# Start bytes of the SBUF tiles in a retention, GLU and SwiGLU kernel: three small edits that shift them

## The chip, the core and the metric

The kernel runs on one core of a Trainium2 chip. The metric is device time in microseconds (us) of one execution. Three runs of the kernel before took 668.92, 669.10 and 670.97 us; their median is 669.1 us. Names used below: PE is TensorE (matmuls), PEld its weight loads, DVE is VectorE, ACT is ScalarE, POOL is GpSimd, SP is the queue that issues most DMAs.

## The reference

Three steps in a row, all in float32:

```
# 1. retention, batch 2, heads 8, sequence 768, head size 64
state = gamma[h] * state + outer(k[t], v[t])
y[t]  = (1 / sqrt(64)) * q[t] @ state
# 2. GLU on x = y as 1536 tokens x 512:  (x @ w_a) * (x @ w_b) @ w_out        (512 -> 1536 -> 512)
# 3. RMS norm with gain rms_g, then SwiGLU: (silu(xn @ w_gate) * (xn @ w_val)) @ w_out
```

## The kernel before

**Retention.** The recurrence is cut into 12 chunks of 128 tokens (6 per batch). A chunk has scores (L363), an update of the state (L379), the part that comes from the state (L389) and the part from the chunk itself (L399). These are float32 matmuls on small tiles. The chunks run first; the last seven are interleaved with the first three units of step 2 (`BETWEEN`), and the last of them is done by 79 us, in group 0.

**The two networks.** A float32 number is split into two float32r numbers, hi and lo, and each product is three float32r matmuls: hi*hi, hi*lo, lo*hi. Each network has 12 slices of 128 hidden features. Of each slice there are three weight pieces (s = 0, 1 for the two up projections, s = 2 for the down projection), 128 x 512 each, held as a `wh` and a `wl` tile. Tokens go in 3 blocks of 512. A *unit* is one slice for one block: two halves of 12 up matmuls (L170 to L172: moving operand `xh` or `xl`, in the second network `nh` or `nl`; stationary operand a 128 x 128 cut of `wh` or `wl`) and 12 down matmuls of an earlier unit. In the first network (L214 to L216) the down weights are stationary and `hh`, `hl` move; in the second (L218 to L220) `hh`, `hl` are stationary and the down weights `wh`, `wl` move. So each unit has 36 matmuls of 512 columns, and there are 72 units, 2592 such matmuls.

**Groups and buffers.** Slices go in groups of 3; a group runs its 3 slices for the 3 blocks, 9 units, before the next begins. There are 8 groups, 0 to 3 in the first network and 4 to 7 in the second. The weight tiles form a ring of six slices. Slices 0, 1, 2 of the ring lie in the pool `wp`, slices 3, 4, 5 ("the last three") in the pool `wq`. Groups 0, 2, 4, 6 read `wp`, groups 1, 3, 5, 7 read `wq`. A down projection runs two to three units behind its up projection, so the first 24 or 36 down matmuls in a group still read the other pool's weights.

**Beside TensorE.** ACT, DVE and POOL turn the raw weights into `wh` and `wl` (`conv_w`; raw loads by SP, the last steps are ACT L136 for `wh` and DVE L138 for `wl`), form `h`, `hh`, `hl` (L194 to L197), and gather the sums (L241 to L245). `norm` (L249 and on) does the RMS norm of a block; it keeps per-token numbers in five tiles of 128 x 4: `me`, `t`, `r`, `rh`, `rl`. POOL spreads `rh` and `rl` into `d` (L278), which PE multiplies with `ones` (L284).

**Order.** The program runs in the order in which it is written. `unit` issues up halves, steps of the conversions and of the norm, and the down matmuls due; `BEGIN` says in which unit a conversion starts. Each engine takes its instructions in that order; waits are for the tiles that an instruction reads or overwrites.

**Where tiles start.** In each partition of SBUF the tiles stand one behind another, pool by pool, each taking its bytes rounded up to 32. The first tile, `rg_sb` (16 bytes), starts at 16,512, a multiple of 128, so the next starts 32 bytes into a line of 128. Nearly all that follow are a multiple of 128 bytes long and keep that. The exceptions are in two places, which use the same memory at different times:

- in the retention's pool `ac`: `dk_sb` (6 x 8 numbers, 192 bytes) and `gq_sb` (6 x 4 numbers, 96 bytes). Behind them stand `warm` and the retention's working tiles `q`, `k`, `qd`, `vd`, `p`, `sd`, `dq`.
- in the pool `yp`, opened when the retention is done: the five norm tiles of 16 bytes, 32 each, 160 in all. Behind them stands `wq`.

| tiles | start before | in a line of 128 |
|---|---|---|
| x and n tiles (`xh`, `xl`, `nh`, `nl`) | 18,080 and on | 32 |
| `wp`: slices 0 to 2 of the ring | 67,232 and on | 32 |
| `g`, `h`, `hh`, `hl`, `raw`, `u`, `v`, `z`, `acc` | 104,096 and on | 32 |
| `sq`, `d` | 175,776 and 183,968 | 32 |
| retention's `q`, `k`, `qd`, `vd`, `p`, `sd`, `dq` | 162,752 and on | 64 |
| `wq`: slices 3 to 5 of the ring | 188,224 and on | 64 |

Of the kernel before, what the change touches and what calls it, by code (L numbers as in the profile page):

```python
# [7 lines left out]
F32 = mybir.dt.float32  # L8
# [7 lines left out]
B, H, S, D = 2, 8, 768, 64  # L16
P = 128
# [5 lines left out]
CPB = S // C  # L23
NP = H // 2
# [3 lines left out]
NB = NT // TB  # L28
CPT = TB // C
TPB = TB // P  # L30
# [9 lines left out]
BEGIN = {0: (1, 1), 1: (1, 1), 2: (0, 1)}  # L40
BEGIN |= {i: (i in (10, 13, 16, 19, 22), 1) for i in (*range(3, 34), *range(39, 66))}
LAG = 3
SIGN = -(1 << 31)

PARTS = KD, TPB
# [3 lines left out]
def retention_glu_swiglu(ctx: ExitStack, tc: tile.TileContext, qk, kv, dq, tri, dk, gq, eye, w1, w2, rg, out):  # L49
# [19 lines left out]
    cst = ctx.enter_context(tc.tile_pool(name="cst", bufs=1))  # L69
# [9 lines left out]
    ones = cst.tile([P, P], F32R, name="ones")  # L79
    ones32 = cst.tile([P, P], F32, name="ones32")  # L80
    ident = cst.tile([P, 1, P], F32, name="ident")

    xs = {}

    def x_tiles(j, what):
        hi = xp.tile([P, KD, TB], F32R, tag="xh", name=f"{what}h{j}")
        lo = xp.tile([P, KD, TB], F32R, tag="xl", name=f"{what}l{j}")
        xs[what, j] = (hi, lo)
# [18 lines left out]
    def conv_w(i):  # L107
# [15 lines left out]
        nc.vector.tensor_scalar(ui, ui, 3, 0x7FFFFFFF, op0=ALU.logical_shift_left, op1=ALU.bitwise_and)  # L123
        nc.vector.scalar_tensor_tensor(ui, upper, SIGN, ui, op0=ALU.bitwise_and, op1=ALU.bitwise_or)
        nc.vector.tensor_scalar(zi, ui, -(1 << 23), None, op0=ALU.bitwise_and)  # L125
# [24 lines left out]
    def step(todo=beside):  # L150
        for g in list(todo):
            if next(g, g) is g:
                todo.remove(g)
# [21 lines left out]
    def up(i):  # L175
# [13 lines left out]
        def second():  # L189
            b = up_half(i, 1)  # L190
            h = hp.tile([P, TB], F32, tag="h", name=f"h{i}")
            hh = hp.tile([P, TB], F32R, tag="hh", bufs=LAG, name=f"hh{i}")
            hl = hp.tile([P, TB], F32R, tag="hl", bufs=LAG, name=f"hl{i}")
            nc.vector.tensor_tensor(h, b, gate[0], op=ALU.mult)  # L194
# [27 lines left out]
    def collect(i):  # L222
        ffn, g, j, f = units[i]
        if f % GRP < GRP - 1:
            return
        if g == 0:
            acc[ffn, j] = (yp if j else y0).tile([P, *((TPB, DM) if ffn else (KD, TB))], F32, tag=f"acc{j}", name=f"acc{ffn}_{j}")
        for m in range(PARTS[ffn]):
            collect_part(ffn, g, j, m)
        if ffn == 0 and g == NG - 1:  # L230
            norming.append(norm(j))
# [17 lines left out]
    def norm(j):  # L249
        y = acc[0, j]  # L250
        sq = yp.tile([P, KD, TB], F32, tag="sq", name=f"sq{j}")
        d = yp.tile([P, 2, TB], F32R, tag="d", name=f"d{j}")
        me, t, r, rh, rl = (yp.tile([P, TPB], F32, tag=w, name=f"{w}{j}") for w in ("me", "t", "r", "rh", "rl"))
        nc.scalar.activation(sq[:, 0:2, :], y[:, 0:2, :], AF.Square)
        nc.scalar.activation(sq[:, 2:4, :], y[:, 2:4, :], AF.Square)
        yield
        yield
        nc.vector.tensor_tensor(sq[:, 0:2, :], sq[:, 0:2, :], sq[:, 2:4, :], op=ALU.add)
        nc.vector.tensor_tensor(sq[:, 0, :], sq[:, 0, :], sq[:, 1, :], op=ALU.add)
        for _ in range(4):  # L260
            yield
        ms = sp.tile([P, TB], F32, tag="S", name=f"ms{j}")
        for c in range(TPB):
            nc.tensor.matmul(ms[:, c:c + 1], sq[:, 0, c * P:(c + 1) * P], ones32[:, 0:1], start=True, stop=True)
        yield

        nc.vector.tensor_scalar(me, ms[:, 0:TPB], 1.0 / DM, 1e-6, op0=ALU.mult, op1=ALU.add)
        nc.scalar.activation(t, me, AF.Sqrt)
        yield
        nc.vector.reciprocal(r, t)  # L270
        nc.vector.tensor_tensor(t, r, r, op=ALU.mult)
        nc.vector.scalar_tensor_tensor(t, t, -0.5, me, op0=ALU.mult, op1=ALU.mult)
        nc.vector.scalar_tensor_tensor(r, t, 1.5, r, op0=ALU.add, op1=ALU.mult)
        nc.vector.tensor_copy(rh.bitcast(F32R), r)
        nc.vector.tensor_tensor(rl, r, rh, op=ALU.subtract)

        for i, w in enumerate((rh, rl)):
            nc.gpsimd.tensor_tensor(d[:, i].rearrange("p (c t) -> p c t", t=P), ident.to_broadcast([P, TPB, P]), w[:, :, None].to_broadcast([P, TPB, P]), op=ALU.mult)  # L278
        yield
        yield  # L280
        yield
        rb = sp.tile([P, TB], F32, tag="S", name=f"rb{j}")
        for i in range(2):
            nc.tensor.matmul(rb, ones, d[:, i], start=(i == 0), stop=(i == 1))  # L284
        yield
        x_tiles(j, "n")
        hi, lo = xs["n", j]
        for e in range(0, KD, 2):
            for k in (e, e + 1):
                nc.vector.scalar_tensor_tensor(y[:, k, :], y[:, k, :], rg_sb[:, k:k + 1], rb, op0=ALU.mult, op1=ALU.mult)  # L290
            nc.scalar.copy(hi[:, e:e + 2, :], y[:, e:e + 2, :])
            yield
            for k in (e, e + 1):
                nc.gpsimd.tensor_tensor(lo[:, k, :], y[:, k, :], hi[:, k, :].bitcast(F32), op=ALU.subtract)
        normed.add(j)
# [3 lines left out]
    def unit(i):  # L299
# [3 lines left out]
        for n, f in enumerate(up(i)):  # L303
# [6 lines left out]
            if n == 0:  # L310
                due(i - (LAG if i < 4 * GRP else LAG2))
                step()

    def due(i):
        while nd[0] <= i:
            for m in range(PARTS[units[nd[0]][0]]):
                down(nd[0], m)
            collect(nd[0])
            nd[0] += 1

    with tc.manual_schedule():

        with ExitStack() as att:
            ac = att.enter_context(tc.tile_pool(name="ac", bufs=1))
# [3 lines left out]

            dq_sb = ac.tile([P, NP, C], F32, name="dq_sb")
            tri_sb = ac.tile([P, 1, C], F32, name="tri_sb")  # L330
            dk_sb = ac.tile([P, CPB, H], F32, name="dk_sb")
            gq_sb = ac.tile([P, CPB, NP], F32, name="gq_sb")
            st = sp.tile([P, B, NP, D], F32, name="st")
            qk_t, kv_t = {}, {}

# [76 lines left out]
            w = ps.tile([P, P], F32, tag="A", name="w")  # L412
# [52 lines left out]
        yp = ctx.enter_context(tc.tile_pool(name="yp", bufs=1))  # L465
# [59 lines left out]
```

## Time and profile before

| | us |
|---|---|
| median of the three runs | 669.1 |
| the profiled execution | 669.5 |
| its span in the trace | 667.7 |
| PE busy in it | 653.4 |
| DVE, ACT, POOL busy | 427.1, 255.6, 166.3 |

The profile is one execution. Busy time of PE is modelled at a matmul's end: neighbouring matmuls are pipelined and their spans overlap (one is drawn about 0.39 us long, the next starts about 0.23 us after it). So for TensorE the distance from start to start is what is read here, over a counted number of matmuls, and not the length of one. Idle time of an engine other than the one that bounds costs nothing by itself.

### The profile page before, as it was taken

What the parts mean: (1) busy time and instruction counts of PE and PEld (TensorE: products, weight loads), DVE (VectorE), ACT (ScalarE), POOL (GpSimd) and SP (SyncE); (2) the same over time, 40 slices, a digit from 0 to 9 for tenths busy, and PEclk for the clock granted to TensorE, in tenths of its full rate; (3) what the DMA queues carried; (4) which work ended last, traced back from release to release, by engine and by line L of the source; (5) the groups of instructions that cost most, each with busy time, mean ns of one, the idle gap of its engine ahead of it and who ended that gap; (6) DMA issues with size and microseconds to landing.
All of it is one profiled execution on the core that took longest, in us unless ns stands there. A gap on an engine that the chain in (4) does not pass through costs nothing.

```text
span 667.7 us, 8594 instructions
## 1 busy us (share of the span) xinstructions
PE 653.4 (98%) x3342; PEld 533.3 (80%) x3342; DVE 427.1 (64%) x703; ACT 255.6 (38%) x436; POOL 166.3 (25%) x118
## 2 busy tenths in 40 slices
PE   7699999999999999999999999999999999999997
PEld 6588888888888888888887888888888888888885
DVE  4988545564876976665765657665665775775333
ACT  3555324444344443333443454443333333332110
POOL 3766211121221222211133225111111111111000
PEclk7899999999999999999999999999999999999999
DMA  9866121231332332222210012122122222200111
GB/s 353 299 234 242 36 64 64 63 96 31 95 95 64 95 95 68 67 61 61 65 60 0 1 31 64 63 64 64 63 64 63 64 63 64 64 31 1 63 64 63
DMA packets 16601, 54.47 MB, mean 82 GB/s; under 512 B 2224, under 2 KB 2736, under 8 KB 16560
## 3 DMA queue, kind: packets, MB, share of 16 engines
q1 hardware_dynamic: 15840, 53.42, 24.8%
q8 instruction: 26, 0.43, 0.3%
q10 hardware_dynamic: 720, 0.50, 0.2%
q14 instruction: 15, 0.12, 0.1%
HBM read 50.76 MB, written 3.15 MB: 81 GB/s over the span
## 4 chain that ended last, share of the span: by engine, by line
PE 91%; DVE 5%; DMA 2%; ACT 1%; POOL 1%; issue 1%; ACTq 0%; DVEq 0%; POOLq 0%
PE a L170 19%; PE a L171 19%; PE a L172 19%; PE y L218 5%; PE y L219 5%; PE y L220 5%; PE y L215 5%; PE y L214 5%; PE y L216 5%; PE ya L399 1%; DMA q<-in_qk 1%; PE ya L389 1%; DMA tri_sb<-in_tri 1%; PE sc L363 1%; DVE acc L241 1%; DVE p L365 1%
## 5 line engine op out<-in xcount | busy, mean ns | idle before, releaser
L126 POOL TENSOR_TENSOR v<-v,z 128x512 f32<-128x512 f32 x72 | 113.2, 1572 | 397.4 <-DVE z L125 397.4
L194 DVE TENSOR_TENSOR h<-a,g 128x512 f32<-128x512 f32 x72 | 49.8, 691 | 154.6 <-PE a L172 154.4
L171 PE MATMUL a<-xl,wh 128*128 128x512 f32 x288 | 113.5, 394 | 0.0
L170 PE MATMUL a<-xh,wh 128*128 128x512 f32 x288 | 113.3, 393 | 0.0
L171 PE MATMUL a<-nl,wh 128*128 128x512 f32 x288 | 113.2, 393 | 0.0
L170 PE MATMUL a<-nh,wh 128*128 128x512 f32 x288 | 113.0, 392 | 0.0
L172 PE MATMUL a<-nh,wl 128*128 128x512 f32 x288 | 112.9, 392 | 0.0
L172 PE MATMUL a<-xh,wl 128*128 128x512 f32 x288 | 112.6, 391 | 0.0
L136 ACT CAST wh<-u 128x512 fp32r<-128x512 f32 x72 | 44.7, 620 | 146.0 <-DVE u L134 145.8
L195 ACT CAST hh<-h 128x512 fp32r<-128x512 f32 x72 | 44.7, 620 | 124.4 <-DVE h L194 124.0
L134 DVE TENSOR_TENSOR u<-u,v 128x512 f32<-128x512 f32 x72 | 53.4, 741 | 28.6 <-POOL v L126 28.6
L170 PEld LDWEIGHTS a<-xh,wh 128*128 128x128 f32 x288 | 54.0, 188 | 13.0 <-issue 0.5
L170 PEld LDWEIGHTS a<-nh,wh 128*128 128x128 f32 x288 | 54.1, 188 | 12.4
L171 PEld LDWEIGHTS a<-nl,wh 128*128 128x128 f32 x288 | 54.1, 188 | 12.2
L172 PEld LDWEIGHTS a<-xh,wl 128*128 128x128 f32 x288 | 54.1, 188 | 12.2
L172 PEld LDWEIGHTS a<-nh,wl 128*128 128x128 f32 x288 | 54.1, 188 | 12.1
L171 PEld LDWEIGHTS a<-xl,wh 128*128 128x128 f32 x288 | 54.1, 188 | 11.8
L138 DVE TENSOR_TENSOR wl<-u,wh 128x512 fp32r<-128x512 f32 x72 | 58.6, 814 | 0.7 <-ACT wh L136 0.7
L215 PE MATMUL y<-hl,wh 128*128 128x512 f32 x144 | 56.8, 395 | 0.0
L197 DVE TENSOR_TENSOR hl<-h,hh 128x512 fp32r<-128x512 f32 x72 | 49.8, 692 | 10.9 <-ACT hh L195 10.7
L218 PE MATMUL y<-wh,hh 128*128 128x512 f32 x144 | 56.6, 393 | 0.0
L219 PE MATMUL y<-wl,hh 128*128 128x512 f32 x144 | 56.6, 393 | 0.0
(71 smaller groups left out, 916.4 us busy)
## 6 DMA issues: line engine op xcount, KB each, us to landing
raw<-in_w SPq DMA_DIRECT2D x72, 512.0 KB, 3.6
q<-in_qk SPq DMA_DIRECT2D x12, 512.0 KB, 5.9
k<-in_kv SPq DMA_DIRECT2D x12, 512.0 KB, 6.1
out<-acc SPq DMA_DIRECT2D x11, 256.0 KB, 2.2
dq_sb<-in_dq ACTq DMA_DIRECT2D x1, 256.0 KB, 4.0
out<-acc SPq DMA_DIRECT2D x1, 128.0 KB, 2.0
out<-acc ACTq DMA_DIRECT2D x1, 128.0 KB, 2.0
tri_sb<-in_tri ACTq DMA_DIRECT2D x1, 64.0 KB, 5.7
```

What stands on the lines that cost most here:

```text
L126: nc.gpsimd.tensor_tensor(v, v, z, op=ALU.mult)
L134: nc.vector.tensor_tensor(u, u, v, op=ALU.add)
L136: nc.scalar.copy(hi, u)
L138: nc.vector.tensor_tensor(lo, u, hi.bitcast(F32), op=ALU.subtract)
L170: nc.tensor.matmul(a, wh[:, c], xh[:, k, :], start=(k == 0), stop=False)
L171: nc.tensor.matmul(a, wh[:, c], xl[:, k, :], start=False, stop=False)
L172: nc.tensor.matmul(a, wl[:, c], xh[:, k, :], start=False, stop=(k == KD - 1))
L194: nc.vector.tensor_tensor(h, b, gate[0], op=ALU.mult)
L197: nc.vector.tensor_tensor(hl, h, hh.bitcast(F32), op=ALU.subtract)
L215: nc.tensor.matmul(y, dh[:, c], hl, start=False, stop=False)
L218: nc.tensor.matmul(y, hh[:, c], dh, start=s, stop=False)
L219: nc.tensor.matmul(y, hh[:, c], dl, start=False, stop=False)
```

## The change

```
@@ -40,6 +40,8 @@
 LAG = 3
+
+LINE = 128
 SIGN = -(1 << 31)
@@ -79,6 +81,7 @@
     ident = cst.tile([P, 1, P], F32, name="ident")
+    small = cst.tile([P, 2 * LINE // 4], F32, name="small")[:, :5 * NB * TPB].rearrange("p (w j t) -> p w j t", j=NB, t=TPB)
@@ -250,7 +253,7 @@
-        me, t, r, rh, rl = (yp.tile([P, TPB], F32, tag=w, name=f"{w}{j}") for w in ("me", "t", "r", "rh", "rl"))
+        me, t, r, rh, rl = (small[:, i, j, :] for i in range(5))
@@ -328,8 +331,8 @@
-            dk_sb = ac.tile([P, CPB, H], F32, name="dk_sb")
-            gq_sb = ac.tile([P, CPB, NP], F32, name="gq_sb")
+            dk_sb = ac.tile([P, LINE // 2], F32, name="dk_sb")[:, :CPB * H].rearrange("p (c h) -> p c h", h=H)
+            gq_sb = ac.tile([P, LINE // 4], F32, name="gq_sb")[:, :CPB * NP].rearrange("p (c n) -> p c n", n=NP)
```

The five norm tiles become cuts of one tile `small` of 256 bytes in the first pool, with a place of its own for each block. `dk_sb` takes 256 bytes and `gq_sb` 128; the numbers in them and the bytes that are loaded stay the same. As a result `wq` starts at 188,320 and the retention's working tiles at 163,104, both 32 bytes into a line of 128. Everything behind `small` moves up by 256 bytes (the x tiles to 18,336, `wp` to 67,488), and keeps its place in a line of 128. No engine's instructions change in number or order. In the built program the waits are the same too, but for `rh` and `rl` of the second and third block: the DVE no longer waits there for POOL to have read those of the block before.

## Rows read from the trace of the kernel before

**Rows 1.** The page: span, PE busy, granted clock by slice, chain by engine
```profile
span 667.7 us, 8594 instructions
...
PE 653.4 (98%) x3342; PEld 533.3 (80%) x3342; DVE 427.1 (64%) x703; ACT 255.6 (38%) x436; POOL 166.3 (25%) x118
...
PEclk7899999999999999999999999999999999999999
...
PE 91%; DVE 5%; DMA 2%; ACT 1%; POOL 1%; issue 1%; ACTq 0%; DVEq 0%; POOLq 0%
```
**Rows 2.** Waits of PE: who for whom, us in total, times, longest
```profile
PE ya L399 <- DVE p L365: 3.3, 2, 3.2
...
PE ms L264 <- DVE sq L259: 0.3, 1, 0.3
```
**Rows 3.** Timeline of PE, start us and us: ends of four stretches of 216 matmuls
```profile
155.04 0.39 PE L214 MATMUL y<-hh,wh 128*128 128x512 f32 x1
...
205.43 0.40 PE L170 MATMUL a<-xh,wh 128*128 128x512 f32 x1
...
230.21 0.39 PE L170 MATMUL a<-xh,wh 128*128 128x512 f32 x1
...
279.18 0.39 PE L170 MATMUL a<-xh,wh 128*128 128x512 f32 x1
...
458.33 0.39 PE L170 MATMUL a<-nh,wh 128*128 128x512 f32 x1
...
508.76 0.40 PE L170 MATMUL a<-nh,wh 128*128 128x512 f32 x1
...
533.47 0.39 PE L170 MATMUL a<-nh,wh 128*128 128x512 f32 x1
...
582.43 0.39 PE L170 MATMUL a<-nh,wh 128*128 128x512 f32 x1
```
**Rows 4.** Timeline of PE: first matmuls of groups 1 and 5, and the last matmul
```profile
127.14 0.39 PE L170 MATMUL a<-xh,wh 128*128 128x512 f32 x1
...
433.18 0.39 PE L170 MATMUL a<-nh,wh 128*128 128x512 f32 x1
...
663.39 0.39 PE L220 MATMUL y<-wh,hl 128*128 128x512 f32 x1
```
**Rows 5.** Windows, groups 5 and 6: length, busy per engine, clock, DMA, GB/s
```profile
433.10:508.70 75.60, 75.60 (x326) 60.87 (x325) 48.37 (x82) 27.79 (x47) 14.48 (x9) 1.00 0.21 63
508.70:582.40 73.70, 73.70 (x325) 60.87 (x325) 48.93 (x84) 26.62 (x45) 14.50 (x9) 1.00 0.22 65
```
**Rows 6.** The same windows for L138 alone, which writes `wl`: DVE busy
```profile
433.10:508.70 75.60, 6.13 (x9) 1.00 0.21 63
508.70:582.40 73.70, 6.14 (x9) 1.00 0.22 65
```
**Rows 7.** Timeline of PE in group 4: two matmuls that read `d`
```profile
394.61 0.62 PE L284 MATMUL rb<-d,ones 128*128 128x512 f32 x2
395.06 0.39 PE L218 MATMUL y<-wh,hh 128*128 128x512 f32 x1
```
**Rows 8.** Timeline of PE: two chunks of the retention between two units
```profile
38.64 1.16 PE L363 MATMUL sc<-qd,q 64*128 64x128 f32 x16
...
46.75 0.50 PE L170 MATMUL a<-xh,wh 128*128 128x512 f32 x1
```
**Rows 9.** Timeline in group 6: the end of a conversion and its first reader
```profile
534.27 0.68 DVE L138 TENSOR_TENSOR wl<-u,wh 128x512 fp32r<-128x512 f32 x1
...
536.41 0.39 PE L219 MATMUL y<-wl,hh 128*128 128x512 f32 x1
```
**Rows 10.** The page, DMA issues: count, KB each, median us to landing
```profile
raw<-in_w SPq DMA_DIRECT2D x72, 512.0 KB, 3.6
q<-in_qk SPq DMA_DIRECT2D x12, 512.0 KB, 5.9
```
**Rows 11.** Groups by line: the norm's cast, busy us, mean ns, idle before
```profile
L274 DVE CAST rh<-r 128x4 fp32r<-128x4 f32 x3 | 0.5, 170 | 0.2
```

## The prediction

> **What bounds the kernel.** I read the page first. PE is busy for 653.4 of 667.7 us, the chain that ended last runs through PE for 91% of its length, and the granted clock is at its full level of 2.4 GHz from the third slice of forty on [rows 1]. Next the waits of PE: they come to a few microseconds, the longest (3.2 us) in the retention's opening; behind 127 us the only one on the list is 0.3 us at the norm [rows 2]. So in the eight groups the time is the number of matmuls times the distance from one start to the next, and anything that changes this distance goes to the end in full.
>
> That distance is the third view. I cut stretches of 216 matmuls (six units), so placed that all their weights come from one pool. Those that read `wp` took 279.18 - 230.21 = 48.97 us and 582.43 - 533.47 = 48.96 us, 226.7 ns per matmul. Those that read `wq` took 205.43 - 155.04 = 50.39 and 508.76 - 458.33 = 50.43 us, 233.4 ns [rows 3]. The difference of 6.7 ns is there in both networks, though in the second the down weights are the moving operand. It isn't company: in groups 5 and 6 the weight loads were equally busy (60.87 us each), POOL 14.48 and 14.50, DVE 48.37 and 48.93, the clock 1.00 in both, and yet group 5 (`wq`) lasted 1.9 us longer [rows 5]. What sets the two pools apart is where they start: `wp` at byte 32 of a line of 128, like every tile that meets it in a matmul, `wq` at byte 64, against moving or stationary partners at 32.
>
> **Part 1: `wq` from byte 64 to byte 32.** After the change the two operands of each of the 2592 matmuls begin at the same byte of a line, as now in the even groups. I take 226.7 ns for all of them and work out each stretch between two starts:
> - groups 1 and 2, from 127.14 to 279.18 us [rows 3, 4]: 660 matmuls in 152.04 us. 660 x 226.7 ns = 149.62. Gain 2.42.
> - groups 5 and 6, from 433.18 to 582.43 us [rows 3, 4]: 648 matmuls in 149.25 us. 648 x 226.7 ns = 146.90. Gain 2.35.
> - group 7 to the last matmul, 582.43 to 663.39 us [rows 3, 4]: 347 steps in 80.96 us. 347 x 226.7 ns = 78.66. Gain 2.30.
> - groups 3 and 4 hold the norm's small matmuls as well, so I take the value of the equal pair 5 and 6: 2.35.
> - group 0 reads `wp` already: nothing.
>
> The sum is 9.4 us. Its lower bound is to take only the 1296 matmuls that read `wq` times 6.7 ns, 8.7 us. The 0.7 between the two are the first matmuls after each change of pool: group 6 as a whole, 508.76 to 582.43 us for 324 matmuls, goes at 227.4 ns, more than its 24 `wq` matmuls explain (24 x 6.7 ns / 324 = 0.5 ns). I take 9.4, since after the change no pair differs.
>
> Two rules of the Trainium skill speak against this. TensorE: Matmul & The Clock Gate, "Step-by-step: what each phase is for", says that the moving operand and the weight load have independent read ports and that loading the next weights takes no read bandwidth from the running matmul. SBUF — State Buffer, "Specifications (TRN2)", gives lines of 16 bytes, of which 32 and 64 are both multiples. By these the start byte would cost nothing and the time stays at 669. The trace disagrees with such a reading of them: 226.7 against 233.4 ns on equal work.
>
> **Part 2: the other engines on `wq`.** DVE writes `wl` in 6.13 us for nine in group 5 (those of the next `wp` group) and 6.14 us for nine in group 6 (those of the next `wq` group) [rows 6]. The start byte is nothing to it, before or after.
>
> **Part 3: the retention's tiles from 64 to 32.** Here both operands of a matmul are at byte 64 before and both at 32 after. If equal bytes are what counts, nothing changes. The trace has no retention matmul with other bytes, so the bound is the networks' ratio: two chunks between two units take 46.75 - 38.64 = 8.1 us [rows 8], the seven interleaved ones some 28 us, and 6.7/226.7 of that is 0.8 us to either side. I take 0. The start of the kernel waits for `q` and `k`, whose landing place moves too. `q` landed in 5.9 us, `raw` of the same size at byte 32 in 3.6 [rows 10]; the `q` loads compete with each other in the opening, which I hold to be the reason. Were it the byte, the first load would come up to 2.3 us earlier. I take 0 and let the low end lean on it.
>
> **Part 4: the norm's tiles.** The DVE loses a wait for POOL in front of `rh` and `rl` of the second and third block. All idle time before the three casts is 0.2 us [rows 11], on an engine that isn't the bound: 0. The instructions themselves are as many as before and 0.17 us each.
>
> **What is late next.** A shorter unit gives its companions less time: 36 x 6.7 ns = 0.24 us. The tightest conversion I found is that of a down piece in group 6: DVE ends it at 534.27 + 0.68 = 534.95 us, and PE reads it at 536.41 [rows 9]. The margin of 1.46 us is six times the loss, and the conversion's order is tied to the unit's own instructions. At the norm PE already waits 0.3 us [rows 2]; there the 0.24 us comes back as a wait, so I add 0.2.
>
> **Sum.** 669.5 (profiled execution; its span is 667.7, and 1.8 lies around it) - 9.4 + 0.2 = 660.3. The profiled execution is 0.4 above the median of 669.1, so I say 660.0.
>
> **The rivals.**
> *The place in the memory counts, not the byte in a line.* `wq` lies at 188,224 and up, `wp` at 67,232. If far addresses are the slow ones, the edits move `wq` by 96 bytes and change nothing: 669.1. This is also what the two pages above would have. For it: all slow slices are both far and at byte 64, so the two aren't parted among weights. Against it: `d` begins at 183,968, byte 32, and two matmuls that read it took 395.06 - 394.61 = 0.45 us, 225 ns each [rows 7], no slower than the fast stretches. Chance 0.07.
>
> *Slower: the place in a longer line counts.* `small` moves everything behind it by 256 bytes. The x tiles and `wp` go from 160 to 416 of a line of 512, `wq` from 320 to 416. If what is slow is not a difference between operands but the upper half of such a line, all 2592 matmuls take 233.4 ns, and the 1296 that read `wp` now cost 6.7 ns more each: +8.7, so 678. It decides as soon as 416 is a slow place. No row of before has a 512-column matmul there. Against it is that cuts of the same weights 512 bytes apart, and tiles 2048 apart, run alike in the stretches of [rows 3], and that a mismatch of the pair accounts for all of the difference. Chance 0.04.
>
> *Part of the gain stays away.* Either the 432 matmuls of the second network whose moving operand is a down piece keep their 6.7 ns in half of them (216 x 6.7 ns = 1.4 us), together with the transition term of 0.7, or late conversions give 0.24 us back in each of the nine units of three groups that have such a tight margin (27 x 0.24 = 6.5 at the very most, 3 as a middle). 662 to 664. Against it: both networks show the same 6.7 ns, and the margin above. Chance 0.09.
>
> **How the numbers follow.** The forecast has a chance of 0.80, with its own range of 658.0 to 662.0: 9.4 with 0.8 for the retention and some for the first load below, 8.7 and a little waiting above. The third rival takes the range up to 664.0. The other two, 0.11 together, stay outside. A time within 0.3% of 669.1 (about what a measurement of this kernel can tell from no change) comes from the first rival alone, 0.07; slower from the second and what I don't see, 0.05; faster is the rest, 0.88.
>
> **What would show it.** If I am right, the 216-matmul stretches of groups 1 and 5 last 48.96 us like those of groups 2 and 6, group 5 lasts about 73.5 us, busy times of DVE, ACT and POOL stay within a few tenths, and the span shrinks to about 658. If groups 1, 3, 5 and 7 still go at 233 ns per matmul, the place and not the byte was the cause; if the even groups rise to 233, it is the longer line. If the stretches are at 226.7 and the time doesn't follow, the waits of PE, above all at L172 and L219, must have grown. It would also be wrong if the retention's stage up to 127 us changed by more than a microsecond.

## The result, and the profile after

The changed kernel took 659.4 us (median of 4 runs, 658.65 to 659.44) against 669.0 us before (median of 4, 668.88 to 670.97). The ratio is 0.9847, 95% interval 0.9828 to 0.9866. 660.0 had been forecast, with a range of 658.0 to 664.0.

The page of the changed kernel, lines as in [rows 1] (span, PE busy, chain by engine):

```profile
span 657.6 us, 8593 instructions
...
PE 643.7 (98%) x3342; PEld 533.2 (81%) x3342; DVE 425.2 (65%) x703; ACT 255.5 (39%) x436; POOL 165.1 (25%) x118
...
PE 92%; DVE 4%; DMA 2%; POOL 1%; issue 1%; ACT 0%; ACTq 0%; DVEq 0%; POOLq 0%
```

The span is 10.1 us shorter and PE is busy for 9.7 us less with the same 3342 matmuls. PE is still the bound. The other engines did the same work in nearly the same time (POOL 165.1 against 166.3, ACT 255.5 against 255.6, DVE 425.2 against 427.1; 1.1 us of DVE's difference is one instruction of the norm, below).

The timeline of PE in the changed kernel (start us, us): the first matmuls of groups 1, 3, 5, 6, 7, and the last matmul. L173 and L223 are L170 and L220 of before:

```profile
126.95 0.39 PE L173 MATMUL a<-xh,wh 128*128 128x512 f32 x1
...
276.55 0.39 PE L173 MATMUL a<-xh,wh 128*128 128x512 f32 x1
...
427.76 0.39 PE L173 MATMUL a<-nh,wh 128*128 128x512 f32 x1
...
501.20 0.39 PE L173 MATMUL a<-nh,wh 128*128 128x512 f32 x1
...
574.64 0.39 PE L173 MATMUL a<-nh,wh 128*128 128x512 f32 x1
...
653.30 0.39 PE L223 MATMUL y<-wh,hl 128*128 128x512 f32 x1
```

Set against [rows 3, 4]: groups 1 and 2 now last 149.60 us (152.04 before), groups 5 and 6 146.88 (149.25), group 7 to the last matmul 78.66 (80.96). Group 5, which reads `wq`, and group 6, which reads `wp`, both take 73.44 us: 324 matmuls at 226.7 ns. Before they took 75.58 and 73.67.

The windows of groups 5 and 6 in the changed kernel (length, busy PE, PEld, DVE, ACT, POOL, clock, DMA share, GB/s), to set beside [rows 5]:

```profile
427.70:501.20 73.50, 73.50 (x325) 60.84 (x325) 47.79 (x82) 27.80 (x47) 14.50 (x9) 1.00 0.21 65
501.20:574.60 73.40, 73.40 (x325) 60.80 (x324) 48.90 (x84) 26.65 (x45) 14.49 (x9) 1.00 0.21 65
```

The same instructions stand in them. The company is as before, and the 1.9 us between the two groups are gone.

### The profile page after: what moved, and what is told of

Its sections match the earlier page's. It is cut to its first block, busy times and chain, and to the rows that moved or that the text cites. A ratio compares the mean times of both kernels' runs of the same rounds, so it can differ in the third digit from the quotient of the medians.

```text
span 657.6 us, 8593 instructions
## 1 busy us (share of the span) xinstructions
PE 643.7 (98%) x3342; PEld 533.2 (81%) x3342; DVE 425.2 (65%) x703; ACT 255.5 (39%) x436; POOL 165.1 (25%) x118
## 4 chain that ended last, share of the span: by engine, by line
PE 92%; DVE 4%; DMA 2%; POOL 1%; issue 1%; ACT 0%; ACTq 0%; DVEq 0%; POOLq 0%
PE a L173 20%; PE a L175 20%; PE a L174 20%; PE y L217 5%; PE y L219 5%; PE y L218 5%; PE y L223 5%; PE y L221 5%; PE y L222 5%; PE ya L402 1%; DMA q<-in_qk 1%; PE ya L392 1%; DMA tri_sb<-in_tri 1%; PE sc L366 1%; DVE p L368 1%; DVE u L126 1%
## 5 line engine op out<-in xcount | busy, mean ns | idle before, releaser
L173 PE MATMUL a<-xh,wh 128*128 128x512 f32 x288 | 112.6, 391 | 0.0
L173 PE MATMUL a<-nh,wh 128*128 128x512 f32 x288 | 112.3, 390 | 0.0
L174 PE MATMUL a<-xl,wh 128*128 128x512 f32 x288 | 112.1, 389 | 0.0
L173 PEld LDWEIGHTS a<-xh,wh 128*128 128x128 f32 x288 | 54.1, 188 | 11.5 <-issue 0.5
L173 PEld LDWEIGHTS a<-nh,wh 128*128 128x128 f32 x288 | 54.1, 188 | 11.1
L141 DVE TENSOR_TENSOR wl<-u,wh 128x512 fp32r<-128x512 f32 x72 | 60.1, 835 | 0.7 <-ACT wh L139 0.7
L217 PE MATMUL y<-hh,wh 128*128 128x512 f32 x144 | 56.0, 389 | 0.0
```

Source lines behind the costliest of these rows:

```text
L141: nc.vector.tensor_tensor(lo, u, hi.bitcast(F32), op=ALU.subtract)
L173: nc.tensor.matmul(a, wh[:, c], xh[:, k, :], start=(k == 0), stop=False)
L174: nc.tensor.matmul(a, wh[:, c], xl[:, k, :], start=False, stop=False)
L217: nc.tensor.matmul(y, dh[:, c], hh, start=s, stop=False)
```

## The experiments

Two theories were set against each other at first. *Pair*: what costs is that the operands of TensorE's matmuls start at different bytes of a line. *Place*: byte 64, or the far memory of `wq`, is slow by itself. Later runs asked how long the line is, how much difference it bears, and which operands have to agree. All edits are to the changed kernel unless said. "Distance" is the start of the shifted weights minus that of the x tiles, of which the remainder after division by 256 is given, since 256 turns out to be the measure. The table gathers the groups 5 (`wq`) and 6 (`wp`), read from timelines like the one above. Each ratio is to executions of the kernel before that were made beside that run (their medians lie between 668.62 and 669.79 us).

| run | distance | group 5, us | group 6, us | time, us | ratio to before (95%) |
|---|---|---|---|---|---|
| before | `wq` 160 | 75.58 | 73.67 | 669.0 | 1 |
| changed | 0 | 73.44 | 73.44 | 659.4 | 0.9847 (0.9828 to 0.9866) |
| small only | 0 | 73.44 | 73.44 | 659.07 | 0.9855 (0.9840 to 0.9870) |
| pads only | `wq` 160 | 75.58 | 73.67 | 668.91 | 1.0002 (0.9993 to 1.0012) |
| all at 64 | 0 | 73.44 | 73.44 | 659.15 | 0.9855 (0.9841 to 0.9870) |
| all at 0 | 0 | 73.44 | 73.44 | 658.87 | 0.9854 (0.9838 to 0.9871) |
| swap | `wp` 32, `wq` 0 | 73.71 | 75.45 | 667.54 | 0.9983 (0.9972 to 0.9994) |
| `wq` + 64 | 64 | 75.34 | 73.65 | 667.99 | 0.9971 (0.9951 to 0.9990) |
| `wq` + 96 | 96 | 75.70 | 73.71 | 670.56 | 1.0011 (0.9999 to 1.0022) |
| `wq` + 128 | 128 | 75.42 | 73.66 | 667.75 | 0.9967 (0.9954 to 0.9981) |
| `wq` + 256 | 0 | 73.44 | 73.44 | 659.72 | 0.9863 (0.9843 to 0.9883) |
| `wq` + 16, mixed | 16 and 144 | 75.16 | 73.55 | 664.92 | 0.9933 (0.9900 to 0.9967) |
| `wq` + 16 | 16 | 74.41 | 73.63 | 662.26 | 0.9901 (0.9881 to 0.9921) |
| lo + 64 | every lo tile 64 from the hi tiles | 74.88 | 74.88 | 671.26 | 1.0039 (1.0024 to 1.0054) |

**The parts of the change.** *Small only*:

```
-dk_sb = ac.tile([P, LINE // 2], F32, ...)[...]      +dk_sb = ac.tile([P, CPB, H], F32, name="dk_sb")
-gq_sb = ac.tile([P, LINE // 4], F32, ...)[...]      +gq_sb = ac.tile([P, CPB, NP], F32, name="gq_sb")
```

> The changed kernel without the longer dk_sb and gq_sb: the weight slices of wq start at byte 32 of a line of 128, the retention's working tiles at byte 64 again. If the pair of operands counts: 659.4 us as with the whole change (within 1), stretches of 216 network matmuls 48.96 us in every group, two retention chunks 8.1 us, since both operands of a retention matmul start alike either way. If byte 64 itself is slow, up to 0.8 us comes back in the retention: 660.2.

659.07 us: the whole gain. The retention's tiles were back at byte 64 of a line of 128. The expectation of 8.1 us for its two chunks between two units was missed: they took 45.85 - 37.17 = 8.68. Timeline of that stretch:

```profile
37.17 1.16 PE L366 MATMUL sc<-qd,q 64*128 64x128 f32 x16
...
40.92 1.16 PE L366 MATMUL sc<-qd,q 64*128 64x128 f32 x16
...
44.24 0.43 PE L402 MATMUL ya<-p,vd 128*64 128x128 f32 x2 [0.52 <-DVE p L368]
...
45.85 0.50 PE L173 MATMUL a<-xh,wh 128*128 128x512 f32 x1
```

The first chunk takes 40.92 - 37.17 = 3.75 us, and 3.75 in the changed kernel too, where the tiles are at byte 32. The excess is a wait of 0.52 us for DVE in the second chunk. Such a wait (0.44 to 0.55 us) stands also in *all at 64* and, with the retention's tiles at byte 32, in `+96` and lo + 64; these four kernels start their networks at 31.5 to 31.8 us, all others, which lack it, at 32.8 or later. So it isn't the pace of the retention's matmuls. *Pads only* is the kernel before with the two longer tiles, and the norm's five tiles as they were:

> The kernel before with the longer dk_sb and gq_sb alone: the retention's tiles at byte 32, the norm's five tiles as before, wq at byte 64. If only the pair of a network matmul counts: 669, odd groups at 233 ns, two retention chunks 8.1 us. If the retention's bytes counted: up to 0.8 us less.

668.91 us, and the groups to the hundredth as before. So one edit of the three carries the change: the norm's five tiles no longer stand between the x tiles and `wq`, which brings these 160 bytes nearer to each other. That they now lie in `small` is not by itself the cause: `+64`, `+96` and `+128` below have them there too and are slow.

**Pair or place.** *All at 64* makes the first tile 64 bytes long:

```
-rg_sb = cst.tile([P, KD], F32, name="rg_sb")      +rg_sb = cst.tile([P, 16], F32, name="rg_sb")[:, :KD]
```

> The changed kernel with the first tile rg_sb 64 bytes long instead of 16: every tile behind it starts at byte 64 of a line of 128. If the difference between the two operands of a matmul counts: 659.4 us, 226.7 ns per matmul in all groups. If byte 64 itself is the slow place: 233.4 ns for all 2592 matmuls, about 677 us (659.4 + 2592 x 6.7 ns = 676.8).

659.15 us: byte 64 isn't slow where all tiles start there. *All at 0* (32 numbers in place of 16):

> The changed kernel with rg_sb 128 bytes long: every tile behind it starts at byte 0 of a line of 128. Pair theory: 659.4 us, 226.7 ns per matmul everywhere. If the place in the line counts by itself, byte 0 may be better or worse than 32: up to 677 if it is like 64, under 659 if an operand that starts with its line is read faster.

658.87 us, the same within its runs (658.41 to 659.30). None of the three places tried (32, 64 and 0 of a line of 128) is better than another. *Swap* puts unused bytes round `wp`:

```
+ctx.enter_context(tc.tile_pool(name="s1", bufs=1)).tile([P, 8], F32, name="s1")
 wps = [ctx.enter_context(tc.tile_pool(name="wp", bufs=1))] * GRP
+ctx.enter_context(tc.tile_pool(name="s2", bufs=1)).tile([P, 120], F32, name="s2")
```

> The changed kernel with an unused 32 bytes ahead of the pool wp and an unused 480 behind it: now wp starts at byte 64 and wq stays at byte 32 (moved by 512 in all), in the same memory regions as before. Pair theory: the even groups become the slow ones, 233.4 ns per matmul that reads wp, the odd ones go at 226.7; group 0 is slow too, so about 669 us. If the far addresses of wq were the cause, nothing changes against the changed kernel: 659.4, or the odd groups are slow.

The timeline of the swapped kernel, first matmuls of groups 5, 6 and 7:

```profile
433.55 0.39 PE L175 MATMUL a<-nh,wh 128*128 128x512 f32 x1
...
507.26 0.39 PE L175 MATMUL a<-nh,wh 128*128 128x512 f32 x1
...
582.71 0.39 PE L175 MATMUL a<-nh,wh 128*128 128x512 f32 x1
```

Now group 6 is the slow one: 75.45 us against 73.71 for group 5. The slowness goes with the mismatch and not with the far memory. Place is out by these three runs. The time, 667.54, is 1.5 under the 669 expected; 0.6 of that lies at the norm (see there), the rest is open.

**How long the line is.** The runs `+128`, `+64`, `+96` and `+256` lengthen the norm's tile `d` by unused bytes, behind which `wq` stands:

```
-d = yp.tile([P, 2, TB], F32R, ...)
+d = yp.tile([P, 2 * TB + 32], F32R, ...)[:, :2 * TB].rearrange("p (a n) -> p a n", a=2)     # 32: +128 bytes; 16, 24, 64 for the others
```

> The changed kernel with wq 128 bytes further (an unused 128 bytes behind the norm's tile d): wq at byte 32 of a line of 128 as the x tiles, but 128 apart from them in a line of 256 or 512. If a line of 128 is what counts: 226.7 ns per matmul in all groups, 659. If a line of 256 or 512 counts: the odd groups slow again, 233 ns, 668.

The timeline with `wq` 128 bytes further, first matmuls of groups 5, 6 and 7:

```profile
432.76 0.40 PE L173 MATMUL a<-nh,wh 128*128 128x512 f32 x1
...
508.18 0.40 PE L173 MATMUL a<-nh,wh 128*128 128x512 f32 x1
...
581.84 0.40 PE L173 MATMUL a<-nh,wh 128*128 128x512 f32 x1
```

Group 5 takes 75.42 us. Here all tiles start at byte 32 of a line of 128, which is what the change set out to do, and all but 0.3% of the gain is gone. A line of 128 is not the measure.

> The changed kernel with wq 256 bytes further. 128 further was slow (232 ns), 512 further (in the swap) was fast. If the start bytes must agree in a line of 256: 226.7 ns per matmul in all groups, 659. If in a line of 512: odd groups at 232 to 234 ns, 668.

The timeline with `wq` 256 bytes further, the same three matmuls:

```profile
427.07 0.39 PE L173 MATMUL a<-nh,wh 128*128 128x512 f32 x1
...
500.51 0.39 PE L173 MATMUL a<-nh,wh 128*128 128x512 f32 x1
...
573.95 0.39 PE L173 MATMUL a<-nh,wh 128*128 128x512 f32 x1
```

73.44 us in both groups. The line is one of 256 bytes: 128 is slow, 256 is fast, and so is 512 (`wq` in the swap, whose groups 5 and 7 are fast but for the matmuls that read `wp`). The change hits it because the 160 bytes behind `d` went away: 188,320 and 18,336 both lie at byte 160 of a line of 256. Before, `wq` lay at 64 of it and the x tiles at 160.

**How much difference is borne.**

> The changed kernel with wq 64 bytes further: operands 64 apart in a line of 128. If any difference within 128 costs: odd groups at 233 ns or another slow value, about 668. If the line is one of 64 bytes: 226.7 ns, 659. If the cost grows with the distance: 13 ns per matmul, about 677.

> The changed kernel with wq 96 bytes further, at byte 0: the weights start 96 above or 32 below their partners in a line of 128. If any difference costs alike: odd groups at 233 ns, about 668. If only the sign of before costs (the loaded weights ahead of the moving operand in the line), the up matmuls go at 226.7 and a gain is kept; if distance counts, up to 20 ns per matmul and 685.

Distances 64 and 96 cost about as much as 32, 128 and 160. Over 215 steps within the first slow group of each kernel, all of whose weights are shifted ones, the pace is 233.3 ns at 32, 233.3 at 64, 234.3 at 96, 232.4 at 128 and 233.3 at 160. The cost doesn't grow with the distance. `+96`, 670.56 us, is 2.6 above its expectation; beside the pace, PE waits 0.9 us there for DVE at the norm's third block, where `+64` waits 0.3 at the second (see the norm below). With 16 bytes there were two runs. The first lengthens each `wq` tile by 128 bytes and cuts the weights 16 bytes into it:

> The changed kernel with each wq tile 128 bytes longer and its weights 16 bytes into it: weights 16 apart from their partners in a line of 128. If the unit that must agree is one of 32 bytes or more, not the byte: 226.7 ns, 659. If any difference of start bytes costs: the odd groups slow, 668.

664.92 us. Its distances are 16 for `wh` and 144 for `wl`, as the line of 256 makes clear only afterwards, so it couldn't answer its question. It holds something else: its group 1 took 203.24 - 127.08 = 76.16 us for 336 matmuls, 226.7 ns, though a third of its up matmuls had weights at distance 144; from group 3 on the odd groups were slow. The second cuts all `wq` weights from one tile:

```
+far.append(wp.tile([P, 6 * GRP * DM + 8], F32R, name="far"))
...
+o = 4 + ((c % RING - GRP) * 3 + s) * 2 * DM
+hi, lo = far[0][:, o:o + DM], far[0][:, o + DM:o + 2 * DM]
```

> The changed kernel with all weights of wq cut from one tile, 16 bytes into it and without gaps, so each starts exactly 16 bytes past its partners in a line of 512 (the run before mixed 16, 144, 272 and 400). If the fast pace is kept until a disturbance, as in the mixed run: group 1 at 226.7 ns, the later odd groups slow after the norm's small matmuls, some 665. If 16 alone is harmless: 226.7 ns throughout, 659. If any difference costs: 668.

The timeline of that kernel in group 3, where the norm of the first block comes in (`far` is `wq`; 12 matmuls between the first two rows, 24 between the last two):

```profile
319.49 0.39 PE L224 MATMUL y<-hh,far 128*128 128x512 f32 x1
...
322.21 0.39 PE L180 MATMUL a<-xh,far 128*128 128x512 f32 x1
...
324.93 0.95 PE L274 MATMUL ms<-ones,sq 128*128 128x1 f32 x8
...
328.62 0.40 PE L224 MATMUL y<-hh,far 128*128 128x512 f32 x1
...
334.22 0.40 PE L180 MATMUL a<-xh,far 128*128 128x512 f32 x1
```

Before the norm's small matmuls the mismatched weights go at (322.21 - 319.49) / 12 = 226.7 ns; after them the same weights go at (334.22 - 328.62) / 24 = 233.3. So there are two paces. With 16 bytes of difference TensorE keeps the fast one that it came with, until a break throws it out, and then keeps the slow one to the end of the group. In the second network, where the down weights move, group 5 lasts 74.41 us, between the two paces, and the pace changes there with no break. The timeline in group 5 (24 up matmuls of mismatched weights, 12 down matmuls, 24 up, 12 down, 24 up):

```profile
441.99 0.39 PE L180 MATMUL a<-nh,far 128*128 128x512 f32 x1
...
447.43 0.39 PE L228 MATMUL y<-far,hh 128*128 128x512 f32 x1
...
450.20 0.39 PE L180 MATMUL a<-nh,far 128*128 128x512 f32 x1
...
455.79 0.39 PE L228 MATMUL y<-far,hh 128*128 128x512 f32 x1
...
458.57 0.40 PE L180 MATMUL a<-nh,far 128*128 128x512 f32 x1
...
464.02 0.39 PE L228 MATMUL y<-far,hh 128*128 128x512 f32 x1
```

The three stretches of up matmuls go at 226.7, 232.9 and 227.1 ns: each block of down matmuls switches the pace, one way and then the other. Why a block does so stays open. The expectation of some 665 was near, 662.26; that of no harm and that of full cost both fell.

**Which operands must agree.** In the last run every lo tile starts 64 bytes past the hi tiles:

```
-lo = xp.tile([P, KD, TB], F32R, ...)
+lo = xp.tile([P, KD * TB + 64], F32R, ...)[:, 16:16 + KD * TB].rearrange("p (k n) -> p k n", k=KD)
-hl = hp.tile([P, TB], F32R, ...)                  +hl = hp.tile([P, TB + 64], F32R, ...)[:, 16:16 + TB]
...
+side, n = c % RING // GRP, (c % GRP * 3 + s) * DM
...
+far[side] = wp.tile([P, 6 * GRP * DM + 64], F32R, name=f"far{side}")
+hi, lo = far[side][:, n:n + DM], far[side][:, 3 * GRP * DM + 16 + n:3 * GRP * DM + 16 + n + DM]
```

> The changed kernel with every lo tile (xl, nl, hl, and wl of both pools) starting 64 bytes past the hi tiles in a line of 256; the weights of each pool are cut from one tile. Matmuls come as hi*hi, lo*hi, hi*lo: two of three now have a moving operand and own weights 64 apart, but the weights that are loaded while a matmul runs, those of the next one, always start like its moving operand. If the pair that must agree is moving operand and next weights (two streams read at the same time): 226.7 ns per matmul in all groups, 659.4. If it is the matmul's own two operands: slow in all groups, 671 to 676 (659.4 + 1728 or 2592 x 6.6 ns).

671.26 us, ratio 1.0039 (1.0024 to 1.0054). Its timeline in group 1 (L176, L177, L178 are hi*hi, lo*hi, hi*lo, the moving operand named first):

```profile
150.22 0.40 PE L176 MATMUL a<-xh,far 128*128 128x512 f32 x1
...
152.30 0.40 PE L176 MATMUL a<-xh,far 128*128 128x512 f32 x1
```

Nine matmuls in 2.08 us are 231 ns, and both networks go at that, but for the stretches with the norm: some 4.4 ns per matmul more, in the even groups too. That the moving operand agrees with the weights loaded meanwhile is not enough, so that theory falls. The time fits the lower end for the matmul's own operands, but all three of the repeating distances from start to start are longer than 226.7 ns (232, 232 and 229), the one whose own operands agree among them. What is shown is that the fast pace stood in every group only where all operands of the stream start alike; by which step of TensorE the mismatch costs stays open.

## Why the prediction was right, point by point

**The pace of the matmuls, -9.4 us: right in size.** The forecast lengths were 149.62 us for groups 1 and 2, 146.90 for 5 and 6, 78.66 for group 7; measured 149.60, 146.88 and 78.66. Groups 3 and 4 went from 154.00 to 151.21 us, 2.79 less, of which 0.50 belongs to the norm (below), so 2.29 where 2.35 had been set. The sum is 2.44 + 2.37 + 2.30 + 2.29 = 9.40. To take the 0.7 us beside the 1296 matmuls into the gain was right. The rest of the 10.1 us that the span lost is the norm's 0.50 and 0.2 ahead of group 1, which is within what that stretch varies from kernel to kernel (126.1 to 128.5 us). The last step of the forecast sum was rounded up: 660.3 less 0.4 is 659.9.

**The reason for it: half right.** That the two operands must begin alike was read from the trace of before and held in *swap*, *all at 64* and *all at 0*. That alike means "in a line of 128" was taken from the change and never tested by a row; `+128` shows it false. The forecast came out because the change also makes the starts agree in a line of 256, and that was luck. With 128 bytes left behind `d`, every tile would have begun at byte 32 of a line of 128 just the same, and my argument would have forecast a gain that `+128` doesn't have. Nor is it shown that each matmul's own two operands are what must agree: in lo + 64 the matmuls whose own operands agree were slow as well.

**The norm, +0.2 us: wrong in sign, -0.5, by luck.** I had the shorter unit come back as a wait. At the norm's second block, in group 3, the wait of 0.3 us for DVE [rows 2] went instead. The timelines of PE, the last network matmul before the norm's small matmuls and the first behind them, before:

```profile
355.84 0.39 PE L172 MATMUL a<-xh,wl 128*128 128x512 f32 x1
...
357.48 0.48 PE L170 MATMUL a<-nh,wh 128*128 128x512 f32 x1
```

and after:

```profile
351.17 0.39 PE L175 MATMUL a<-xh,wl 128*128 128x512 f32 x1
...
352.21 0.49 PE L173 MATMUL a<-nh,wh 128*128 128x512 f32 x1
```

That is 1.64 us before and 1.04 after, 0.60 less. The timelines of DVE and POOL show why, before:

```profile
354.67 1.29 POOL L294 TENSOR_TENSOR nl<-acc,nh 128x512 fp32r<-128x512 f32 x1 [3.03 <-ACT nh L291]
...
354.68 1.83 DVE L259 TENSOR_TENSOR sq<-sq 128x512 f32<-128x512 f32 x1
```

and the same two instructions of the changed kernel:

```profile
350.24 1.83 POOL L297 TENSOR_TENSOR nl<-acc,nh 128x512 fp32r<-128x512 f32 x1 [3.03 <-ACT nh L294]
...
350.25 0.69 DVE L262 TENSOR_TENSOR sq<-sq 128x512 f32<-128x512 f32 x1
```

The two start within about 0.01 us of each other. Where DVE lost, its sum of squares took 1.83 us and PE waited for it; where it won, it took 0.69, and POOL's instruction 1.83 in place of 1.29. The Trainium skill (SBUF — State Buffer, "SBUF: two separate sides") has DVE with two SBUF inputs and POOL share a pair of ports that whoever starts first holds for the whole instruction. The rows agree with it in that one of the two is delayed, DVE by 1.14 us and POOL by 0.54, either 0.15 less than the other's instruction takes undelayed; that the first to start wins they don't show, since POOL's start is recorded first either way. Over the second and third blocks of all fourteen traces POOL leads by 0 to 5 ns where DVE won and by 6 to 11 ns where it lost. At the second block *pads only*, `+64`, `+128` and the second `+16` show 1.83 or 1.84 us as before, all others 0.69. So 0.6 us hung on a few nanoseconds that the change didn't set out to move.

At the third block, in group 4, DVE won both times, and there the shorter unit did come back as a wait. The last network matmul, the small matmuls' weight load and the next network matmul, in the changed kernel:

```profile
377.06 0.39 PE L175 MATMUL a<-nh,wl 128*128 128x512 f32 x1
...
377.29 0.97 PEld L267 LDWEIGHTS ms<-ones,sq 128*128 128x128 f32 x8 [0.26 <-DVE sq L262]
...
378.20 0.48 PE L173 MATMUL a<-nh,wh 128*128 128x512 f32 x1
```

and the two matmuls before:

```profile
382.56 0.39 PE L172 MATMUL a<-nh,wl 128*128 128x512 f32 x1
...
383.60 0.47 PE L170 MATMUL a<-nh,wh 128*128 128x512 f32 x1
```

1.14 us against 1.04: 0.10 of the 0.24 that had been forecast. The net is -0.50.

**The retention, 0 with 0.8 to either side: right.** The two chunks between units took 8.1 us before, in *pads only* and after; the 8.7 of *small only* is a wait, as shown above. The first network matmul started at 32.98 us before and at 32.93 after. Over all traces this start lies between 31.5 and 33.2 us, at 31.49 in *small only* with the tiles at byte 64 and at 33.06 in *pads only* with them at 32, so one trace of each can't show what the landing place of the first loads is worth below some 1.5 us; no gain of it was seen.

**The conversions: right.** DVE's nine writes of `wl` took 6.15 and 6.14 us in groups 5 and 6, against 6.13 and 6.14 before [rows 6]. The waits of PE after are those of the opening alone; the first lines of that list in the changed kernel (who for whom, us in total, times, longest):

```profile
PE ya L402 <- DVE p L368: 3.3, 2, 3.2
PE st L382 <- DVE vd L358: 2.0, 1, 2.0
```

**The rivals.** Far memory fell with *swap*. The upper half of a line of 512 as the slow place fell with the changed kernel itself, where all tiles lie at 416 of such a line, and any absolute place with *all at 64* and *all at 0*, which put them at 448 and at 0 at the same pace. Its idea that the line is longer than 128 was the sound part of it. The part gain didn't come. The two pages of the Trainium skill that were read as speaking for no effect (TensorE: Matmul & The Clock Gate, "Step-by-step: what each phase is for", on independent read ports; SBUF — State Buffer, "Specifications (TRN2)", on lines of 16 bytes) don't carry that reading: distances of 32 to 160 bytes, all multiples of 16, cost 5.7 to 7.6 ns per matmul. Whether the ports themselves meet each other no run shows, since the step that costs stays open.

## What to carry to other kernels

Where TensorE is the bound and loads new weights for every matmul, give the tiles that it streams and the tiles that it loads the same start byte in a line of 256. A small tile whose length isn't a multiple of 256 shifts everything behind it, so collect small tiles in one or pad them. The runs show this for float32r matmuls of 512 columns; other types and lengths weren't tried. To find such a loss, compare the distance from start to start over a counted number of matmuls between buffers that do the same work; the busy share, 98% before and after, hides it. An alignment that a change names should be tested at twice its length before it is believed.

## What the runs showed of the hardware that was not expected

- The line is one of 256 bytes in all runs of the table: at distance 0 (or 256, or 512) 226.7 ns per matmul of 512 float32r columns, at 32, 64, 96, 128 and 160 some 232 to 234. The 144 of the first `+16` run, in a third of the up matmuls, cost nothing as long as the pace stayed the fast one.
- The pace has a memory. At a distance of 16 bytes both 226.7 and 233.3 ns were held for long stretches by the same weights; in the first network a break in the stream moved TensorE from the one to the other, in the second the blocks of down matmuls did.
- After a block of mismatched weights the matched ones are back at 226.7 ns within a few matmuls: 3 or 4 in group 6 of before, 8 in its group 5. After the norm's small matmuls the changed kernel needs some 10. Group 6 of before took 73.67 us and not 73.44 mainly because of its 24 down matmuls that read `wq` (2.81 us per 12 in place of 2.72), and for the rest because of this settling.
- Two instructions of DVE and POOL that start within about 0.01 us of each other are worth 0.6 us to PE at the norm's second block, depending on which of them is held up. In `+96` and `+128` DVE lost at the third block, and PE waited 0.9 us for it.
